# A new table of order, engines and buffers for a two-layer attention kernel

## The chip, the cores and the metric

The kernel runs on one core of one Trainium2 chip. The metric is the device time of one execution in microseconds (us), as the median of several runs. Engines are named as in the profile: PE (matrix multiplication; PEld is its weight load), ACT (activations), DVE (vector), POOL (GpSimd) and SP (which here only issues DMAs).

## The reference, cut to what matters

Four residual layers in a row work on one sequence x of 2048 tokens by 512 features in bf16, with 32 heads of 16 features. Layers 1 and 3 are "A", layers 2 and 4 are "B", with the same weights each time.

```python
x = x + A(layernorm(x)); x = x + B(layernorm(x)); x = x + A(layernorm(x)); x = x + B(layernorm(x))

def A(x, wq, wk, wv, wo, beta):          # four segments of 512 tokens
    for s in range(4):
        p = softmax(qs @ ks.T / 4 + causal mask)          # inside the segment
        a_mem = (phi(qs) @ M) / (phi(qs) @ z + 1e-6)      # memory of the segments before
        o = sigmoid(beta) * a_mem + (1 - sigmoid(beta)) * (p @ vs)
        M = M + phi(ks).T @ vs;  z = z + sum(phi(ks))     # phi(t) = t+1 if t>0 else exp(t)
    return concat(o) @ wo

def B(x, wqkv, w_phi, wo):
    q, k, v = split(x @ wqkv)
    f = lambda t: concat(softmax(t @ w_phi), softmax(-(t @ w_phi)))
    kv = f(k).T @ v;  z = sum(f(k))                       # over all 2048 tokens
    return (f(q) @ kv) / (f(q) @ z + 1e-6) @ wo
```

## The kernel before, in words

The Python code records about 2900 operations in a graph: loads, layer norms, projections, scores, exponentials, evacuations, transposes. Each operation knows what it reads and writes, which engines could run it, and which buffers of which pool it opens. An operation on PE is a group of matmuls (4 to 32 of them), on the other engines one instruction as a rule.

Work is tiled by 128 tokens (a tile) and by 512 tokens (a segment of A, a chunk of B). In A, `a_proj` makes keys, queries and values of a segment: `pair` at L341 splits a projection into two groups of 8 matmuls with 512 columns each (weights `WA_q`, `WA_k`, `WA_v`; on the way out `WA_o`; in B `WB_q`, `WB_k`, `WB_v`, `WB_o`). These are the wide matmuls of the text. `a_att` makes the scores (`D<-pK,pQ`, the diagonal ones with a mask from `tri,rep`), the exponentials on ACT at L351 (`p<-D`, `pP<-D`), and the product with the values (`D<-pW,p` and `D<-pW,pP`, at most 50 columns). All of these and the small products of B (`D<-Rz`, `D<-Rkv`, `D<-MSb`) go through `mm` at L326. The small products are the narrow matmuls of the text. `D` is PSUM: four buffers of 128x1024 f32 that everything PE writes has to share.

B has a barrier of data: `b_query` needs the sums over the keys of all four chunks, which `kv_add` collects. So each B layer has a stretch of wide projections, then `Rz` and `Rkv` products, exponentials and divisions. The next A layer starts on the first tiles that come out.

Transposes are of two kinds. Most are DMAs that SP issues at L364 (`pX<-p` for a normalised input, `p<-p` for an attention output). Those in `PE_T` are done by PE at L380 and evacuated by ACT (L359) or DVE (L360).

Before the first data arrive, PE runs 100 matmuls on a constant (L701, `warm`, `D<-onesb`). Their results are used by nothing.

What sets the order is a table, `ORDER`: a packed list that gives, for all operations, one global order; for each operation its engine; for each buffer its number in its pool. `Graph.place` unpacks it, and `Graph.emit` writes each engine's stream in that order with the semaphore waits that the dependencies and the buffers' reuse need. Nothing reorders at run time: an engine that waits holds up all that stands behind it, and SP's DMAs are issued in the written order too.

```python
raw = zlib.decompress(base64.b85decode("".join(table.split())))
order = [self.ops[i] for i in np.frombuffer(raw, "<u2", n)]
slots = dict(zip(tiles, raw[3 * n:]))
for k, o in enumerate(order):
    o.seq, o.eng = k, ENGS[raw[2 * n + o.id]]
```

Of the kernel before, what the change touches and what calls it, by code (L numbers as in the profile page):

```python
# [16 lines left out]
D = 512  # L17
H = 32
# [42 lines left out]
class Tile:  # L61
# [236 lines left out]
class Kernel:  # L298
# [908 lines left out]
c-q~01C%YvvUWtIvs$OSk8RtwZQHhO+qP}nwr$&fRlCpJnYnk?y!+O_-oMs;xqDYuRz^lfeDOu>tkrRVL1IV_0QI0g5Hx^>&<LVIV`u_Rp&2xXWDp(VLOiGjnV~wAhxkweBxHk<Py<Rq  # L1207
R%ih&p%o~o3AvyGRD^<12y#MeXal987PN&jPzl;W3@8f;pfD7H_Rs-pLs38|1~H*Bl!M~X5n@3d=mec1AtZwAkOQhfUFZ!dAr)BY0=Xdxe1{+K6RN^%2!uD_Krr-yx6l_1e1z067}CHX
0PG3_;3**Xhj-8qy1@__3Q6G^aOe&LAvfm1_wWfm!xtC@d9erdgo%(3d%-l!iNhcl22lp^1H$z%12@2Q3`c`dz)YMA&*23O#t9GvmOemn%m}&IJa`GOU?Y^kuP_|Oz$WO2{V|wAXex|`
qF4+^!Z%m~4n=}3Fb#&_e8|E!!*&<}L(z}6LP?wsJ760`qX9SvRzWHBCx**lCuD)yFbQYEK->iyRs+XbFc||eEzE!^7=%k9I*o<Xum;NGR1|1&5|qUPxEzXLK`e|FFdXK`wJ;3JVLm8>  # L1210
XQ4E%gF?6hD&k5Qj`MH?#-K_V4#vTJ91j675+}oc9EDThFzkl|cmy1bKnLI;B*f7eKt~}MBhnr?2{CCe&cWTV4`*Q_j75>i4`<^7*b9j<KkS1EI0iGpSk$O+F)YO;I2RjW6I_gouo^bR
g_sVSVpLd()$u$mz{6-TB}OKRXJ8fXqKP;T7r}Tez?R{1Jc3nlH>JWxSQ%?z3P_Dru`$NRwOA9Qz(qJf>o5vkfJ+buS5bXT$7*41tcwew9yZ5=6c^LOYKo76R0mt&IoOOXu^G0)E!Y}Q
;wjvSo6sMUV0es&$MFQV!M1n^{4oTh(sc->qZoh@@CNLm^SA@EvIH0rFW@oUircXr?xo|f4WnZkTtk=P3be<A7!5-)Hm#-b)B$(nYCMN~Fa{ojLwFX~;Ck$cJ@5>6!VTD(R$wGNjXg0L
uArTmo@HQdXcxxBmb8*mP-pCd4e26Y!pIm4yJCGxj@>XNMa5Rsi1twpN<}HK0bRzV7>D*#FYJwduqL&o+EkZnQ9FuDQLqjbWc6qX#iQJ;J6?q=cnvyJV!A;$X(@G~tGJ0aQv$k%*YPek
rzX^xhEgXQM$M=%wx=6-6K`P%+<|-8fjUwP8crjqDRrf5^cd4(H@c74X(Yv`6EKRN-~-HxPcb9Dz=!w@vtcGIK$-C+X2;&thk8;kDoCeb5GAB#G=Y{=dc2K~Fas8%@$?+W&^Q`MqbVJB
r~cHJ22ej*M`I}om7pWEo`%q1I!YVp4i=`8l!x7djg*Z|q)C*Wm7-&GoDNYA)`Jey7D`H~X&X(Zt@Ie4KoR<ciRc}D#*8d4drx0*I~8Kz@fGI4T=W+2P(GHM^3V@FOH=48zM<E+gU--h
+DRv<Fnde)=p@~z+famEp=30bp3!M4%F@s&x=P>h9G$02G>x9qbh=Ep=n%`qa<bc$kKW@0I?O&%F?vK<@Dlq>KauDuy}`@uF{Put^om~72TV^#*hf6d($YivK}G2+eW3jGg)&eFmYIE|
($tY9r@`zA{iGpmAmfyuU1NjT3lcPsGSWM|&fM}vFX;xGPYdWKW7L&(W8dfkNy-b~Nzp~hN(WeR%0$4BX<A6xs4O#dkPT%g*f3U(on&RHCmYE|u@P(r^<v#wZ$@l58^g-89;_l8&B{|5
%1*b~ZN}IDR)J2jiqwboW96tX%L6&75@n%dtUo)=j<cCGi)Pb4wx1PaIcO}q!ZK5FHjZ6ol6PWfSP7>1ImX#Nc8AR&!S1tCtTL5klD%R6>>+!=?y^Pnmd$04*hMyvy<&4IfZc>D^q9S7
# [80 lines left out]
```

## Time and profile before

| what | value |
|---|---|
| runs | 456.90, 456.93 and 458.73 us, median 456.93 us |
| span of the profiled execution | 454.8 us |
| PE, PEld, DVE, ACT, POOL busy | 427.2, 289.5, 403.1, 420.9, 58.4 us |
| PE's granted clock | 1.000 over the span |
| instructions | 26184, of them 12085 matmuls and 12085 weight loads |

The profile tells the profiled execution's time as its span, from the first to the last instruction of the program. The median run is 2.1 us longer than this span; that is taken as what lies around the span.

A row of the waits reads: engine, tile and line that waited, what released it, microseconds in total, how often, the longest. A row of the timeline reads: start, length, engine, line, operation, tiles and shape, how many were merged, and in brackets the idle time just before with its releaser. "issue" as releaser means that the engine waited for nothing that the profile shows. A row of the windows reads: the stretch, its length, then for each engine the busy time and in brackets the number of its instructions that lie in it, the clock, the share of DMA and its rate.

### The profile page before, as it was taken

To read this page: it belongs to the slowest core of one execution; us is meant where nothing else is said; L and a number is where in the kernel's file an instruction comes from. 1 tells how busy PE (TensorE), PEld (TensorE's weight loads), DVE (VectorE), ACT (ScalarE), POOL (GpSimd) and SP (SyncE) were. 2 spreads that over 40 slices of the span, in tenths; PEclk is the share of its full clock that TensorE was granted. 3 is DMA by queue.
4 is the path that set the end of the run, shared out by engine and by line. 5 is a ranking of instruction groups with operands and counts; after the bars stand their busy time and mean duration, and the time that the engine had idled before them with its cause. 6 is when DMAs were issued, how large, how long until landed. Compare 5 with 4: busy or idle time off the path is not lost.

```text
span 454.8 us, 26184 instructions
## 1 busy us (share of the span) xinstructions
PE 427.2 (94%) x12085; PEld 289.5 (64%) x12085; DVE 403.1 (89%) x766; ACT 420.9 (93%) x584; POOL 58.4 (13%) x146
## 2 busy tenths in 40 slices
PE   8999999999999989989999998999999988999787
PEld 4756667767766666655556666677677666765444
DVE  7999999998798978869999997999898896788897
ACT  5999999999999997899999999999899999699992
POOL 3411014010101101100330112020020020110000
PEclk9999999999999999999999999999999999999999
DMA  8976655564247212101255668436232414300355
GB/s 251 217 165 100 99 93 109 107 87 80 45 76 111 38 40 50 13 3 27 62 111 86 85 97 103 71 87 81 57 50 49 109 19 63 46 17 4 49 91 180
DMA packets 105167, 36.71 MB, mean 81 GB/s; under 512 B 91730, under 2 KB 105058, under 8 KB 105058
## 3 DMA queue, kind: packets, MB, share of 16 engines
q1 hardware_dynamic: 104226, 34.50, 42.9%
q8 instruction: 95, 1.56, 1.4%
q10 hardware_dynamic: 800, 0.52, 0.4%
q14 instruction: 14, 0.11, 0.1%
q0 software_dynamic: 32, 0.02, 0.0%
HBM read 10.76 MB, written 6.55 MB: 38 GB/s over the span
## 4 chain that ended last, share of the span: by engine, by line
PE 61%; ACT 20%; DVE 12%; issue 3%; DMA 3%; POOL 1%; DVEq 0%
PE D L341 38%; PE D L326 22%; ACT p L351 11%; ACT pP L351 7%; DVE X L961 2%; DVE pQ L686 1%; DVE p L1117 1%; DVE stats L599 1%; DMA pX<-p 1%; DMA p<-p 1%; ACT pS L351 1%; DVE p L620 1%; DMA X<-in_A_x_dram 1%; DVE pK L360 1%; DVE p L906 1%
## 5 line engine op out<-in xcount | busy, mean ns | idle before, releaser
L351 ACT ACTIVATE p<-D 128x1024 bf16<-128x1024 f32 (+1 forms) x256 | 225.6, 934 | 10.8 <-PE D L341 4.9
L351 ACT ACTIVATE pP<-D 128x640 bf16<-128x640 f32 (+2 forms) x192 | 149.5, 828 | 7.2 <-PE D L326 5.9
L326 PE MATMUL D<-pK,pQ 64*128 64x128 bf16 (+6 forms) x1792 | 112.0, 227 | 4.2 <-ACT p L351 1.0
L326 PEld LDWEIGHTS D<-pK,pQ 64*128 64x128 bf16 x1792 | 67.0, 93 | 40.2 <-ACT pP L351 8.5
L326 PE MATMUL D<-pW,pP 64*128 64x50 bf16 (+1 forms) x3072 | 84.0, 181 | 3.4 <-issue 2.7
L326 PEld LDWEIGHTS D<-pW,pP 64*128 64x128 bf16 x3072 | 68.6, 93 | 9.2 <-issue 3.8
L607 POOL TENSOR_SCALAR rstd<-mv 128x1 f32<-128x1 f32 x60 | 17.0, 288 | 340.8 <-DVE mv L600 340.4
L326 PE MATMUL D<-pW,p 64*128 64x50 bf16 (+1 forms) x2048 | 50.4, 181 | 0.4 <-DVE pQ L686 0.2
L326 PEld LDWEIGHTS D<-pW,p 64*128 64x128 bf16 x2048 | 44.3, 93 | 3.9 <-issue 1.1
L599 DVE BATCH_NORM_STATS2 stats<-X 128x6 f32<-128x512 bf16 x63 | 42.3, 679 | 1.9 <-DMA X<-in_A_x_dram 1.6
L961 DVE TENSOR_TENSOR X<-X,D 128x1024 bf16<-128x1024 bf16 (+1 forms) x36 | 39.2, 1096 | 5.1 <-PE D L341 4.6
L326 PE MATMUL D<-tri,rep 64*128 64x64 bf16 (+1 forms) x384 | 40.1, 197 | 0.0
L341 PE MATMUL D<-pX,WA_k 64*128 64x512 bf16 (+1 forms) x288 | 37.4, 353 | 1.0 <-issue 0.5
L341 PE MATMUL D<-pX,WA_q 64*128 64x512 bf16 (+1 forms) x288 | 37.7, 353 | 0.6 <-issue 0.6
L609 POOL TENSOR_TENSOR rstd<-rstd,mhalf 128x1 f32<-128x1 f32 x60 | 35.9, 604 | 3.4
L341 PE MATMUL D<-WB_k,pX 64*128 64x512 bf16 (+1 forms) x288 | 33.8, 352 | 1.1 <-DMA pX<-p 0.4
L341 PE MATMUL D<-WA_o,p 64*128 64x512 bf16 (+1 forms) x288 | 33.2, 352 | 1.6 <-issue 0.8
L1015 DVE TENSOR_REDUCE pS<-p 128x64 f32<-128x1024 bf16 x28 | 33.4, 1211 | 0.9 <-ACT p L351 0.9
L341 PE MATMUL D<-WB_v,pX 64*128 64x512 bf16 (+1 forms) x288 | 33.3, 352 | 0.0
L341 PE MATMUL D<-WA_v,pX 64*128 64x512 bf16 x256 | 33.2, 377 | 0.0
L341 PE MATMUL D<-WB_o,p 64*128 64x512 bf16 (+1 forms) x288 | 32.5, 353 | 0.4 <-ACT p L351 0.3
L341 PE MATMUL D<-pX,WB_q 64*128 64x512 bf16 x256 | 32.5, 376 | 0.3 <-ACT p L351 0.3
(123 smaller groups left out, 665.5 us busy)
## 6 DMA issues: line engine op xcount, KB each, us to landing
v_rows<-pV SPq DMA_DIRECT2D x16, 272.0 KB, 3.6
pW<-v_rows SPq DMA_DIRECT2D x64, 68.0 KB, 2.7
out_dram<-X SPq DMA_DIRECT2D x7, 256.0 KB, 2.6
X<-in_A_x_dram SPq DMA_DIRECT2D x3, 512.0 KB, 7.7
pX<-in_B_wqkv_dram SPq DMA_DIRECT2D x3, 512.0 KB, 4.5
p<-p SPq DMA_TRANSPOSE x73, 3.2
pX<-p SPq DMA_TRANSPOSE x54, 3.6
WA_k<-in_A_wk_dram SPq DMA_DIRECT2D x2, 256.0 KB, 7.2
```

What stands on the lines that cost most here:

```text
L326: ins = e.matmul(out_ap, lhsT, rhs, start=st, stop=sp, tile_position=(basep(lhsT), basep(out_ap)))
L341: ins = e.matmul(out_ap, lhsT[64 * hf:64 * hf + 64], rhs[64 * hf:64 * hf + 64], start=k == 0 and i == 0, stop=k == 1 and i == len(lists[hf ...
L351: return self.g.op({"act": (dur, lambda e: e.activation(out_ap(), in_ap(), func, scale=scale))}, reads, writes, opens, label=label)
L360: "dve": ((340 if fast else n / 0.96 + 65), lambda e: e.tensor_copy(out_ap(), in_ap()))}
L599: v(lambda e: e.bn_stats(self.stats[:, t, :], self.X[:, t, :]), 602, [R("X", t)], [R("st", t)], label="bn")
L607: v(lambda e: e.tensor_scalar(rs, self.mv[:, t, 1:2], LN_EPS, None, op0=ALU.add), 170, [R("mv", t)], [R("rstd", t)], eng="pool", label="rstd")
L609: v(lambda e: e.tensor_tensor(rs, rs, self.mhalf[:], ALU.pow), 540, [R("rstd", t), R("mhalf")], [R("rstd", t)], eng="pool", label="rstd")
L620: v(lambda e: e.tensor_scalar(xn.t[:], self.X[:, t, :], self.mv[:, t, 0:1], self.rstd[:, t:t + 1], op0=ALU.subtract, op1=ALU.mult), 300, [ ...
L686: ch = {"dve": (129 + n / 3.84, lambda e, sl=sl, out=out: e.tensor_scalar(out(), src(), self.m4[:, sl:sl + 1], None, op0=ALU.mult))}
L906: v(lambda e, pvv=pvv, rden=rden, part=part: e.tensor_tensor(part(o).rearrange("p (a h d) -> p a h d", a=2, h=16), pvv()[:, :, :, 0:16], r ...
L961: self.v(lambda e: e.tensor_tensor(X(), X(), src(), ALU.add), 65 + 512 * n / 0.96, pr + xr, xr, label="res")
L1015: v(lambda e, E=E, k=k, Z=Z: e.tensor_reduce(Z.t[:, 64 * k:64 * k + 64], E.t[:].rearrange("p (a f h) -> p a h f", a=16, h=4), AX.X, ALU.ad ...
```

## The change

Only the table `ORDER` is replaced. The code around it and the operations are the same.

```diff
 ORDER = """
-c-q~01C%YvvUWtIvs$OSk8RtwZQHhO+qP}nwr$&fRlCpJnYnk?y!+O_-oMs;xqDYuRz^lfeDOu>tkrRVL1IV_0QI0g5Hx^>&<LVIV`u_Rp&2xXWDp(VLOiGjnV~wAhxkweBxHk<Py<Rq
...
+c-q}q1DGvIvd)M|SG)V#wr$(CZQHhO+qP}nw(VEvoI5i+v-4(mpT2Kjoi1c$X5f!MqB1)+OT?10WGoI#z_PGtEGi?$SZ0=xNtTU8XGvIMmXpP0@mPG8hh=5CSUHxRWn#ryc~*iUE5Hh}s;nBT&PuWx
...
 """
```

On the large scale the order stays: the same layers, segments and chunks follow each other in the same way, and groups move by a few places. Twenty operations change their engine. From ACT to DVE go three evacuations of transposed inputs, one evacuation of a value projection of B, two of transposed outputs and two maskings of keys; from DVE to ACT go four evacuations (one of keys, one of queries, one of values, one of a transposed output) and one masking. Seven memsets and fills move between POOL and DVE, all in the first 25 us.

At the start of PE's stream, the warm-ups (`onesb`) before the change are spread between the four transposes of normalised inputs (`ident,p`) and the first projections:

```order
L701 MATMUL D<-onesb 128x256 x8
L380 MATMUL D<-ident,p 128x64 x8
L701 MATMUL D<-onesb 128x512 x4
L380 MATMUL D<-ident,p 128x64 x8
L701 MATMUL D<-onesb 128x512 x2
L380 MATMUL D<-ident,p 128x64 x8
L701 MATMUL D<-onesb 128x512 x4
L380 MATMUL D<-ident,p 128x64 x8
L341 MATMUL D<-pX,WA_k 128x256
```

After it, at the same place:

```order
L701 MATMUL D<-onesb 128x256 x8
L701 MATMUL D<-onesb 128x512 x18
L380 MATMUL D<-ident,p 128x64 x8
L701 MATMUL D<-onesb 128x512 x2
L380 MATMUL D<-ident,p 128x64 x8
L701 MATMUL D<-onesb 128x512 x4
L326 MATMUL D<-beta_sb,onesb 128x32
L380 MATMUL D<-ident,p 128x64 x16
L341 MATMUL D<-pX,WA_k 128x256
```

Nine groups of warm-ups now stand ahead of the first transpose, and none is left between the first projections, where eight matmuls of them stood.

The second place is PE's stream in the third segment of the second A layer, around 321 us of the profile. Before, 52 narrow matmuls in one piece, two diagonal scores, 12 more narrow ones, and then the projection of queries:

```order
L326 MATMUL D<-pW,pP 128x50 x52
L326 MATMUL D<-pK,pQ 128x192 x2
L326 MATMUL D<-pK,pQ 128x64 x2
L326 MATMUL D<-pK,pQ 128x128 x2
L326 MATMUL D<-tri,rep 128x2x32 x2
L326 MATMUL D<-pK,pQ 128x224 x2
L326 MATMUL D<-pK,pQ 128x96 x2
L326 MATMUL D<-pK,pQ 128x128 x2
L326 MATMUL D<-tri,rep 128x2x32 x2
L326 MATMUL D<-pW,pP 128x50 x12
L341 MATMUL D<-pX,WA_q 128x512 x8
L326 MATMUL D<-pK,pQ 128x256 x4
```

After, in PE's stream at the same place:

```order
L326 MATMUL D<-pW,pP 128x50 x64
L341 MATMUL D<-pX,WA_q 128x512 x8
L326 MATMUL D<-pK,pQ 128x224 x2
L326 MATMUL D<-pK,pQ 128x96 x2
L326 MATMUL D<-pK,pQ 128x128 x2
L326 MATMUL D<-tri,rep 128x2x32 x2
L326 MATMUL D<-pW,pP 128x50 x20
L326 MATMUL D<-pK,pQ 128x256 x4
L341 MATMUL D<-pX,WA_q 128x512 x8
```

The first half of the projection (eight wide matmuls) has moved up, so that 16 wide matmuls instead of 8 stand within the same count of matmuls.

The third place is SP's queue where it issues the transposes of the first chunk's input of B (`pX1`) between 63 and 82 us. Before:

```order
L364 DMA_TRANSPOSE pX1<-p14 128x4x128
L364 DMA_TRANSPOSE pX1<-p16 128x4x128
L462 DMA pX2<-in_B_wqkv_dram 128x4x512
L364 DMA_TRANSPOSE pX0<-pX2 128x4x128
L368 DMA pW1<-v_rows 32x8x136 x2
```

After:

```order
L364 DMA_TRANSPOSE pX1<-p10 128x4x128
L462 DMA WB_o<-in_B_wo_dram 64x1x512
L364 DMA_TRANSPOSE pX1<-p12 128x4x128
L368 DMA pW1<-v_rows 32x8x136 x2
L364 DMA_TRANSPOSE p11<-p25 128x4x128
L462 DMA WB_o<-in_B_wo_dram 64x1x512
```

A load of a weight piece now stands between the first two of the four transposes.

More of the change, by code (lines that the diff above doesn't have):

```diff
@@ L1211 @@
[L1211 to L1218, printed above, removed]
@@ L1259 @@
[L1259 to L1261 removed]
+c-q}q1DGvIvd)M|SG)V#wr$(CZQHhO+qP}nw(VEvoI5i+v-4(mpT2Kjoi1c$X5f!MqB1)+OT?10WGoI#z_PGtEGi?$SZ0=xNtTU8XGvIMmXpP0@mPG8hh=5CSUHxRWn#ryc~*iUE5Hh}s;nBT&PuWx
@@ new lines @@
+tQ4!s3bDehG^@ZWvRbSNQw&&LR*%(Z4Om0gh&5(SSX0)FHD@hYOV*0DW^Gto){eDj9au-!iFIaOSXb7Km0{gkQPzX?WGPr#mXcLsm04|8hgl|=VVngphZSSJSZ~&c#bBD{U{zQu_KkgKAJ|70ll@=}
+2C_kHFzd^PFo1rnKO4Yau_x>``@}x8H|#AN$uh9?>?wQ4azIWf0_)g%RusmwTrd@K!!$q$WD!^p3t{is2KJ2QXV2MaHi5lh8`&H-8K%QrHU(zDJT{6=VPDvAHjyo6shPzfe95A)uWTyI19_nYY-7cs
+Burx?STN3JW7tv_6_>E$&=<C|i9pZ~CczH2k}YF7X*uJth^=BPn1JMLFa*L7*vz)DO>8UM$<DG+wwvu@d)Qv)&(5%5HkQp~7J^_L8^(sRU~q6Xi-rTC5R`&4P#T6p0muhsAwQIZNvt50hr%$K4T8Ba
+4A!vzFb@Vm1*iyX*+>`;huC4ZkL_o(m;*=Hd^UqkXCq(~%!UN80usU;2!WO02M1VY%0-DlLVhw(fKD+5;ZZ{<oMzE62FAp+l!YSTJ{SWNU<vGpnJ^2+!Xh{Xdtfn)gT^o#4nq^z3n`!~%!m3=4I02s
@@ new lines @@
+91ja&0fb;EW@LW2fGve(P#Jb%N@xhxp$asD8W0OoK}5_=kuWReW&7~}HiMP83Y$Y378%pBFw8>*sSstO+-xE9$Jh`D(ouTKKx?2b)P@$&6k5V2SPQM79@K)GPzQEnYiI-cSUPrr#e<{lBHIjmFfN3H
+OKby#hhuP=9b^$85*%ZZAppZ58pMaZ6afAZktK$6tP-4O$-$3B!6eWYVqsE94dE~lmqRkx2*=?BY=L!f63)X}*bZA^HLi!<a1M6C5jX?e-~g<_qi_(SLOZy|uCw;g0an2&I1S5jHLSoExD$3jOKgR$
+F*<aF3vdy-Ll5W#Q6M?i!}{0&Q{Y}~i2JZQc7~qN1$seB><Yah23&%)kPf;*IMxT!LmG$)v9Si$#5Pz9>tI`qgS9atEXFJBDqDglSzU~aiSROX!uHq<ui_QBhRty!UWHBA5j$f$ypBz=F*d<QI1D@B
+Be;P>a5xUd$B+Rs!W~G6Cs-HkikaXp6s8`S1+qdmxCYPR3G~GLI0AcN0elKCU?ld&dvG5T-~-4`*P$SG!y9lDvO{9bNVgz0_Q$a}9+%=M?1!Uq9QMHhxE2TEGAxdLaUCAUF*q0p;SpSqC2#^x#7P*L
@@ new lines @@
+-Dct0LpX_>@exack6Ao?3CCG{d<GlvC~m`&7{(&8+t3{gVPTw%$M7I-!PmGQKf)(Cgl{kveui)G1-?U0%!NBJ4d%wTcpBf~DZGux@eF>%yLbmb;XT}nC-5>}!72C@pW#$|13v)qEWUzsm<Oj}UVIH-
+VJ>C{hWU{2JkG=UxBwsFO?;0J@jJeQ4|oeN;tza+kMR<|#P^UEU*SRe0EZ|YUZhKu9>3sye2$;-0lvV)#PJ9XqQR5}1$LpYc%8oC4eCloC<hhAWSA67VJ0eu7w{&_N15?00G7rgC{f{6(zu_l(E(bB
+jDV)2!Ayvh6|-R(8bIx-2bHCP)RQ_;IXX_mXao(X{xpO}Qa?ID-DoJ4#|n6oy3;8dMZKsu9i=`rn)=dB%7_&x16IT_G?r%IOq_+s=oS^Fy(IZQQoI-yr`cEu%is-G4$I;q%#K7ka1P#Lm+1lBr*m|d
+t`Mht)RAt}9ePQxNKh$~RFYoPLpnnjXbwH5v-F1MQe`|(^Qa0gpwl#;6jen{{!|T1ljb#PAsNp3BYHxDPoRlZi=NUm3ZN-8mC92n849EzvQ(Qo(Nda3%V{!oreF%Ah!l<@(JY!x57;!CPRq#h#Wa&<
@@ L1262 @@
+!(|XEm+zsj8gHdQ3URY300KQWl4ocrC+&_1Ca)-R*%<0V;$es<6<rO=pS+L0I_ZKzzMZw#1W)FLdad&<Vm*GjCCj>$)h?!fKX>0QLkzmff!=ID9_Sb1#xvMMO<z)IcV;LH@MM6;6W2GF7_Rh?K<>ig
+#xoGT+R006S8I^<8bCgyQMj3G!d#t}0z7rb11hl)*D;RDTLauvt6&UuD}@BFPLE{)ZiM~3g~R)bT*qaor^*EhuRd?O8jC#GgIADiBRGoOY81#J#3<KPZz%i%JTqM>VdR<TMpc63TDWFom>XC($lO&8
+j<FH~6$Wc2J?IHeDg?RlWQk>NF>@f;o0A^?y1C=h{XYOp&F7Z
 """
```

82 lines of the change are left out of this document (36 added, 46 removed).

## The prediction

> **What bounds the kernel now.** I read the page first: busy shares, the chain that ended last, the DMA queues.
>
> ```profile
> span 454.8 us, 26184 instructions
> PE 427.2 (94%) x12085; PEld 289.5 (64%) x12085; DVE 403.1 (89%) x766; ACT 420.9 (93%) x584; POOL 58.4 (13%) x146
> q8 instruction: 95, 1.56, 1.4%
> PE 61%; ACT 20%; DVE 12%; issue 3%; DMA 3%; POOL 1%; DVEq 0%
> ```
>
> PE and ACT are both about full, and the chain changes between them: 61% of it is PE, 20% ACT. All operations stay, so only waits can go. The third row is the one to remember: a queue of the kind "instruction" moved 95 packets. PE's stream is 12085 weight loads, 12085 matmuls and some 140 waits, and 95 times 256 is 24320. So one packet carries about 256 instructions of PE, or 128 matmuls with their loads. I call that a block.
>
> Second, the waits of PE's two rows of work.
>
> ```profile
> PEld D L326 <- ACT pP L351: 10.4, 34, 1.1
> PEld D L326 <- ACT p L351: 9.7, 29, 0.8
> PEld D L326 <- issue: 8.8, 17, 1.7
> PEld D L341 <- issue: 8.8, 23, 1.0
> PE D L326 <- issue: 4.9, 7, 1.6
> PE D L341 <- issue: 2.5, 5, 0.8
> ```
>
> Weight loads stand still for 20.1 us because an exponential is late, and for 17.6 us, 40 times, on "issue": nothing that the profile shows holds them. Queued matmuls cover most of that; 12 such stalls reach the matmuls and make 7.4 us of idle PE. Third, the timeline of PE shows where these stand.
>
> ```profile
> 162.52 0.61 PE L341 MATMUL D<-pT,p 64*128 64x68 bf16 x28 [0.33 <-issue]
> 203.57 0.21 PE L326 MATMUL D<-Rz,p 64*128 64x32 bf16 x4 [0.46 <-issue]
> 260.24 0.80 PE L341 MATMUL D<-pX,WA_k 64*128 64x512 bf16 x5 [0.52 <-issue]
> 281.12 0.27 PE L326 MATMUL D<-pW,pP 64*128 64x50 bf16 x8 [0.78 <-issue]
> 323.54 0.37 PE L341 MATMUL D<-pX,WA_q 64*128 64x512 bf16 x1 [0.62 <-issue]
> 386.03 1.34 PE L341 MATMUL D<-WA_o,p 64*128 64x512 bf16 x8 [0.84 <-issue]
> 424.77 0.24 PE L326 MATMUL D<-Rz,p 64*128 64x48 bf16 x7 [1.55 <-issue]
> ```
>
> They fall inside a group of equal matmuls, between two that wait for the same things: the queries' projection is cut after seven of eight at 323.54. Fourth, the windows that end at a stall, with one that has none.
>
> ```profile
> 162.51:166.52 4.01, 3.09 (x128) 2.43 (x128) 2.98 (x3) 3.56 (x6) 0.00 (x0) 1.00 0.20 40
> 200.58:203.56 2.98, 2.06 (x140) 1.84 (x132) 1.86 (x5) 2.81 (x5) 0.00 (x0) 1.00 0.02 5
> 256.24:260.23 3.99, 3.48 (x129) 2.75 (x128) 3.96 (x8) 3.89 (x6) 0.00 (x0) 1.00 0.65 85
> 276.98:281.11 4.13, 3.05 (x134) 2.21 (x129) 3.45 (x10) 3.91 (x5) 1.12 (x3) 1.00 0.87 126
> 319.80:323.53 3.73, 3.12 (x129) 2.39 (x128) 3.59 (x7) 3.33 (x5) 0.79 (x2) 1.00 0.46 90
> 396.00:418.00 22.00, 22.00 (x374) 14.21 (x371) 19.29 (x35) 20.27 (x32) 1.57 (x4) 1.00 0.12 15
> ```
>
> The first window runs from one stall to the next and holds 128 matmuls and 128 loads, one block. The next four were laid over one block each, counted in PE's order; each ends in a stall after 3.0 to 4.1 us. So the next block is not there sooner than that, and PE stands when its work for 128 matmuls is shorter. Such a block is one with few wide matmuls. This bounds PE from outside, and moving matmuls between blocks changes it. The last window, without stalls, is a B layer's projections: PE is never idle there, ACT is.
>
> [...]
>
> **The change, part by part.** First, the start.
>
> ```profile
> 1.11 5.58 PE L701 MATMUL D<-onesb 64*128 64x512 bf16 x76 [1.11 <-DVE onesb L531]
> 7.39 0.29 PE L380 MATMUL D<-ident,p 64*128 64x64 bf16 x8 [0.69 <-DVE p L620]
> 9.24 0.27 PE L341 MATMUL D<-pX,WA_k 64*128 64x256 bf16 x1
> ...
> 13.42 0.38 PE L701 MATMUL D<-onesb 64*128 64x512 bf16 x2
> ...
> 214.04 1.03 PE L341 MATMUL D<-WB_o,p 64*128 64x512 bf16 x8
> 214.91 0.63 PE L326 MATMUL D<-Rkv,p 64*128 64x64 bf16 x32
> ...
> 4.43 0.69 DVE L599 BATCH_NORM_STATS2 stats<-X 128x6 f32<-128x512 bf16 x1 [1.57 <-DMA X<-in_A_x_dram]
> ...
> 12.41 1.33 ACT L688 ACTIVATE pQ<-p,m 128x512 bf16<-128x512 bf16 x2
> 14.30 2.23 ACT L351 ACTIVATE pP<-D 128x768 bf16<-128x768 f32 x3
> ```
>
> A matmul of 512 columns takes 0.109 us (eight of them from 214.04 to 214.91). The 76 warm-ups end at 6.69 by their row; 18 more take 2.0 us behind them, less the last one's modelled tail of some 0.2. So the first transpose starts at about 8.4, not 7.39. Behind it six warm-ups stand instead of ten, and two of the evacuations go to DVE beside ACT, so I put the first projection at about 9.5 instead of 9.24. From there the 64 projection matmuls ran 4.18 us, to 13.42, with six of the eight warm-ups between (0.65; the last two are the row at 13.42); without them they end at about 13.0: 0.4 us sooner. ACT masks one key block there instead of two (1.33 us for both, so 0.62 us less ahead of its evacuation). The first exponential moves from 14.30 to about 13.6. **Start: -0.7 us**, between 0 (the loads then set the pace) and -1.2. The memsets that change engine lie ahead of DVE's first input at 4.43, where it waits 1.57 us for data; that hides them. Without that cover the gain of the start would be lost to them: the end 0.
>
> Second, the blocks. The price of a narrow matmul from spacing in the timeline:
>
> ```profile
> 281.45 0.26 PE L326 MATMUL D<-pW,p 64*128 64x50 bf16 x8
> 281.55 0.23 PE L326 MATMUL D<-pW,pP 64*128 64x50 bf16 x6
> ```
>
> Eight wide ones take 0.87 us, eight narrow ones 0.10 (281.45 to 281.55): eight wide ones in place of eight narrow ones make a block 0.77 us longer. In the new order the block that ended in the stall at 203.57 has 8 wide ones for none, that at 260.24 has 19 for 12, that at 281.12 has 8 for none, that at 323.54 has 16 for 8. Each gains about what its stall was, so I take these four as gone: 0.46 + 0.52 + 0.78 + 0.62 = 2.4 us. At 386.03 four value products and a score now stand ahead of the `WA_o` group, which also waited for its data: 0.4 of the 0.84 us. The blocks at 162.5, 166.5 and 424.8 are as short as before (none, 8 and none wide): their stalls stay. In the count of all 94 whole blocks, 17 instead of 18 have under ten wide ones and 6 instead of 9 have under four. Four others get longer and four get shorter by a group; the worst new one stands before 218 us (8 for 16) and could stall for some 0.6 us, the mean of the twelve. I set these against each other. PE then loses 2.8 us less.
>
> Does PE's time reach the end? In the four windows ACT was busy 2.81 of 2.98, 3.89 of 3.99, 3.91 of 4.13 and 3.33 of 3.73 us: it has only 0.9 us of room there. What PE gains beyond that waits for ACT next, unless it is used in stretches like 396 to 418, where PE alone sets the pace and ACT had 1.7 us to spare. Ends: -0.9 (ACT's room alone), and -4.3 (the 17.6 us of load stalls shrink by a quarter, as the time by which blocks fall short of 3.6 us does, from 21 to 17 us by these prices). **Blocks: -2.4 us**, nearer to the four rows than to the estimate over all.
>
> Third, the engines. Behind the start, four evacuations leave ACT and four come.
>
> ```profile
> L359 ACT ACTIVATE pX<-D 128x512 bf16<-128x512 bf16 x10 | 5.7, 596 | 1.3 <-PE D L380 1.3
> ...
> L359 ACT ACTIVATE pV<-D 128x1024 bf16<-128x1024 f32 x3 | 3.2, 1064 | 0.0
> ```
>
> Two of those that come have 1024 columns (1.06 us each), one of those that leave; the other five have 512 and are near 0.6. ACT's work changes by about +0.5 us and DVE's by as little, and I set **0**, ends -0.5 and +0.5. At the end of the kernel PE's groups are the same: 0.
>
> Sum: -0.7 - 2.4 + 0 = -3.1 us against the span of 454.8, so 451.7. The runs' median lies 2.1 us above the span, so 456.93 - 3.1 = **453.8 us**.
>
> **The rivals.**
>
> More: all load stalls shrink, -0.7 - 4.3 - 0.5 = -5.5, 451.4 us. For it speaks that the relieved blocks lie in both A layers; against it that most load stalls are covered. ACT takes over: PE waits as long for `p` and `pP` as it waited for instructions. Then only ACT's room counts: -0.9 and half the start, 455.7 us. For it: the 20.1 us. Against it: 61% of the chain is PE. [...]
>
> Slower: a transpose comes late in SP's queue.
>
> ```profile
> 66.28 4.52 DMA pX<-p
> 70.89 1.04 PE L341 MATMUL D<-WB_k,pX 64*128 64x512 bf16 x8 [0.41 <-DMA pX<-p]
> 21.20 0.67 SPq L462 DMA_DIRECT2D WB_o<-in_B_wo_dram  x1
> 82.95 1.19 SPq L364 DMA_TRANSPOSE p<-p  x1
> ```
>
> SP issues in the written order, a transpose takes it 1.2 us, and the key projection at 70.89 already waited for one. In the new order a load of 0.67 us stands between the two transposes that this group needs, so it would start at about 71.6. Elsewhere, a needed transpose behind one more transpose comes 1.2 us later. Three of these uncovered eat the gain of 3.1; from five on the kernel is over 0.5% slower: -3.1 + 5 x 1.2 = +2.9, 459.8 us. For it: many transposes stand in another order. Against it: of all PE rows shown, this is the only one told to have waited for a DMA, and it waited 0.41 us, so elsewhere there is cover.
>
> **How the numbers follow.** Forecast 0.43, more 0.13, ACT 0.22, the page's rule 0.07, slower 0.15. What a measurement of this kernel can tell from no change is about 0.5%, 2.3 us: under 454.6 is faster, over 459.2 slower. Forecast and more are faster (0.56), ACT and the rule the same (0.29), slower 0.15. The range reaches from a little under the case "more", 450.3, to the case "slower" without its last places, 458.6; it leaves out the tails of these two. The forecast's own range is 452.5 to 455.3 (blocks from -0.9 to -3.7).
>
> **What would show each step.** Right: fewer than 12 stalls of PE's matmuls on "issue", about 5 us together, none in the groups named, those at about 162, 166 and 424 still there; the first `pP` exponential at about 13.6. Wrong: "issue" falls while the waits for `p` and `pP` grow by as much (ACT); a new stall just before 218; PE's waits for `pX<-p` or `p<-p` over 3 us (slower). The prediction is wrong as a whole if PE's stalls move to other blocks instead of going.

## The result and the profile after

| | time | runs |
|---|---|---|
| before | 457.31 us median (456.90 to 458.73) | 4 |
| after | 472.79 us median (472.58 to 477.32) | 4 |
| forecast | 453.8 us, range 450.3 to 458.6 | |

The change makes the kernel slower: ratio 1.0362, 95% interval 1.0307 to 1.0417, about 16 us. The span of the profiled execution grew from 454.8 to 471.0 us. The page after, the rows that answer to those of before:

```profile
span 471.0 us, 26155 instructions
PE 437.7 (93%) x12085; PEld 283.3 (60%) x12085; DVE 404.1 (86%) x774; ACT 421.3 (89%) x581; POOL 54.2 (12%) x141
q8 instruction: 95, 1.56, 1.4%
PE 65%; ACT 13%; DVE 12%; DMA 4%; SPq 3%; issue 3%; DVEq 0%
```

The work of ACT and DVE is nearly what it was; both have more idle time. PE is busy 10.5 us longer with the same 12085 matmuls. The chain has 4 points more of PE, 7 less of ACT, and SP's queue is in it now. The waits of PE, after:

```profile
PEld D L341 <- PE D L341: 27.1, 66, 0.6
...
PEld D L326 <- ACT p L351: 9.5, 25, 1.3
PEld D L326 <- ACT pP L351: 8.9, 31, 0.7
PEld D L341 <- issue: 8.9, 23, 1.5
...
PEld D L341 <- DMA pX<-p: 5.4, 4, 3.7
PEld D L326 <- DMA pW<-v_rows: 3.6, 3, 1.8
PEld D L326 <- issue: 3.5, 12, 0.5
...
PE D L341 <- issue: 1.8, 3, 0.8
...
PE D L326 <- issue: 0.6, 2, 0.4
```

and two rows of the same view before, which the prediction had not shown:

```profile
PEld D L341 <- PE D L341: 2.2, 5, 0.6
...
PEld D L341 <- DMA pX<-p: 0.6, 2, 0.3
```

The forecast gain is there: idle time of PE's matmuls on "issue" fell from 7.4 us in 12 stalls to 2.4 us in 5. It is even larger than these rows tell, because "issue" also stands where the view names no releaser. Counted through PE's stream (weight loads, matmuls and the waits that are instructions of their own), 11 of the 12 stalls before stand 189 to 192 instructions behind a multiple of 256: these are stalls at block borders, 7.1 us in sum. After, only three stand there, 0.8 us. The other two are at groups that wait for a transpose: 0.77 us at 75.52, where it landed at 75.43, and 0.79 us at 79.43, where it landed at 79.34.

But the first row is new. PE's weight loads wait 66 times for PE's own matmuls, where they waited 5 times before. In `pair`, the second half of a projection adds to the same part of `D` as the first half, from the other 64 rows of the array, so `hard=o1` makes it wait until the first half has ended. No run here leaves the wait out of this form, so the traces show its price, not what it is needed for. Before, another group stood between the halves 153 times in 158, and hid the wait; after, 66 second halves stand directly behind their first. The timeline shows what that costs:

```profile
95.76 1.04 PE L341 MATMUL D<-WA_o,p 64*128 64x512 bf16 x8
96.86 1.04 PE L341 MATMUL D<-WA_o,p 64*128 64x512 bf16 x8
```

The second half starts 1.10 us after the first; eight wide matmuls took 0.87 (the prediction's rows at 214.04 and 214.91). So a direct pair (a second half right behind its first) costs 0.23 us, and 61 more of them some 14 us.

Where the time was lost shows in the first and last start of the same groups, before and then after (minimum, median and maximum duration in ns, first and last start in us):

```profile
L341 PE MATMUL D<-WA_o,p x288: 266/376/387, 54.7 to 399.4; 64*128 64x512 bf16 x112, 64*128 64x256 bf16 x32
L341 PE MATMUL D<-pX,WB_q x256: 372/376/387, 177.1 to 430.7; 64*128 64x512 bf16 x128
```
```profile
L341 PE MATMUL D<-WA_o,p x288: 267/376/387, 60.3 to 413.7; 64*128 64x512 bf16 x112, 64*128 64x256 bf16 x32
L341 PE MATMUL D<-pX,WB_q x256: 372/376/387, 185.0 to 447.0; 64*128 64x512 bf16 x128
```

The new kernel is 5.6 us late at 55 us, 7.9 at 177, 14.3 at 399 and 16.3 at 431: a loss at the start, and then one spread over the whole kernel. The matmuls themselves did not become slower (376 ns in both).

**The start.** Windows before and after, first of the kernel before and then of the new one (the count in brackets after PE's busy time is that of its matmuls):

```profile
2.00:4.00 2.00, 2.00 (x12) 0.68 (x10) 0.86 (x1) 1.13 (x1) 1.81 (x8) 1.00 0.94 292
4.00:6.00 2.00, 2.00 (x50) 1.09 (x48) 1.54 (x5) 1.51 (x4) 0.00 (x0) 1.00 0.85 239
```
```profile
2.00:4.00 2.00, 2.00 (x12) 0.74 (x10) 1.94 (x7) 1.13 (x1) 1.54 (x5) 1.00 0.94 289
4.00:6.00 2.00, 2.00 (x12) 0.77 (x10) 1.97 (x9) 1.74 (x5) 0.00 (x0) 1.00 1.02 290
```

Until 4 us both run the wide warm-ups at one in some 0.2 us, half the later speed, though the granted clock is told as 1.00. Before, this ended at 4.0 us; in this execution of the new kernel it went on to 6.2. Then the rows of PE, ACT and SP, after, and SP before:

```profile
1.15 8.58 PE L701 MATMUL D<-onesb 64*128 64x512 bf16 x94 [1.15 <-DVE onesb L531]
9.56 0.28 PE L380 MATMUL D<-ident,p 64*128 64x64 bf16 x8
...
28.57 1.04 PE L341 MATMUL D<-pX,WA_k 64*128 64x512 bf16 x8 [3.48 <-ACT p L351]
...
15.54 1.72 ACT L351 ACTIVATE pP<-D 128x896 bf16<-128x896 f32 x2
...
13.72 1.28 SPq L364 DMA_TRANSPOSE pX<-p  x1
...
19.36 1.23 SPq L364 DMA_TRANSPOSE pX<-p  x1
...
21.27 1.34 SPq L364 DMA_TRANSPOSE pX<-p  x1
...
23.63 1.27 SPq L364 DMA_TRANSPOSE pX<-p  x1
```
```profile
12.38 1.29 SPq L364 DMA_TRANSPOSE pX<-p  x1
...
14.89 3.58 SPq L364 DMA_TRANSPOSE pX<-p  x2
...
19.25 1.91 SPq L364 DMA_TRANSPOSE pX<-p  x1
```

The first transpose of PE starts at 9.56 instead of 7.39. DVE's two evacuations wait for it, the next segment's layer norm stands behind them, and its four transposes are issued up to 23.63 instead of 19.25. PE's `WA_k` group at 28.57 then stood 3.48 us. The row names ACT's `p`, but the exponential that the group waits for had ended at 24.8; the group's other waits are for the four transposes, the last of which landed at 28.4.

**A balance of PE's time.** Over all 1165 groups I took the spacing from each group's start to the next, less the lower quartile for its kind (398.4 us in sum). The rest I put down to what the next group waited for, or to the inside of the group. In us, for runs told of below as well:

| kernel | own first half | inside a group | waits with a DMA among them | ACT | DVE | other |
|---|---|---|---|---|---|---|
| before | 1.1 | 19.1 | 8.5 | 13.3 | 9.4 | -0.1 |
| after | 15.2 | 8.1 | 17.0 | 17.6 | 7.1 | 2.9 |
| a_sep | 0.7 | 14.9 | 17.6 | 23.2 | 14.3 | 2.6 |
| a_pe | 7.6 | 10.4 | 13.5 | 21.4 | 9.1 | 1.7 |
| a_three | 6.0 | 13.4 | 14.0 | 19.9 | 9.2 | 1.2 |
| b_shift | 1.2 | 34.5 | 8.6 | 14.5 | 10.1 | 3.5 |

After against before: +14.1 for the halves, -11.0 inside groups (the block stalls, and load stalls that reach matmuls), +8.5 at waits that have a DMA among them, +4.3 ACT, -2.3 DVE, +3.0 other: +16.6 us. The balance is accounting, not a cause; the runs below test the causes.

### The profile page after: what moved, and what is told of

Read it like the earlier page. It is cut to its first block, busy times and chain, and to the rows that moved or that the text cites. A ratio compares the mean times of both kernels' runs of the same rounds, so it can differ in the third digit from the quotient of the medians.

```text
span 471.0 us, 26155 instructions
## 1 busy us (share of the span) xinstructions
PE 437.7 (93%) x12085; PEld 283.3 (60%) x12085; DVE 404.1 (86%) x774; ACT 421.3 (89%) x581; POOL 54.2 (12%) x141
## 4 chain that ended last, share of the span: by engine, by line
PE 65%; ACT 13%; DVE 12%; DMA 4%; SPq 3%; issue 3%; DVEq 0%
PE D L341 41%; PE D L326 21%; ACT p L351 8%; ACT pP L351 4%; SPq L364 3%; DMA pX<-p 3%; PE D L701 2%; DVE p L835 1%; DVE X L961 1%; ACT pS L351 1%; DMA p<-p 1%; DVE p L1117 1%; DVE pT L360 1%; DVE p L906 1%; DVE pQ L686 1%
## 5 line engine op out<-in xcount | busy, mean ns | idle before, releaser
L351 ACT ACTIVATE pP<-D 128x768 bf16<-128x768 f32 (+2 forms) x192 | 148.9, 818 | 11.4 <-PE D L326 9.8
L326 PE MATMUL D<-pK,pQ 64*128 64x128 bf16 (+6 forms) x1792 | 109.3, 227 | 3.3 <-ACT pP L351 1.9
L326 PE MATMUL D<-pW,pP 64*128 64x50 bf16 (+1 forms) x3072 | 85.0, 181 | 3.6 <-DMA pW<-v_rows 2.8
L326 PEld LDWEIGHTS D<-pK,pQ 64*128 64x128 bf16 x1792 | 64.4, 93 | 34.5 <-ACT pP L351 6.1
L607 POOL TENSOR_SCALAR rstd<-mv 128x1 f32<-128x1 f32 x60 | 14.7, 249 | 354.7 <-DVE mv L600 354.6
L326 PE MATMUL D<-pW,p 64*128 64x50 bf16 (+1 forms) x2048 | 49.0, 181 | 0.9 <-ACT pP L351 0.4
L326 PEld LDWEIGHTS D<-pW,p 64*128 64x128 bf16 x2048 | 43.3, 93 | 3.5 <-issue 1.1
L609 POOL TENSOR_TENSOR rstd<-rstd,mhalf 128x1 f32<-128x1 f32 x60 | 34.7, 585 | 3.5
```

Of the source, the lines that this page charges most:

```text
L326: ins = e.matmul(out_ap, lhsT, rhs, start=st, stop=sp, tile_position=(basep(lhsT), basep(out_ap)))
L351: return self.g.op({"act": (dur, lambda e: e.activation(out_ap(), in_ap(), func, scale=scale))}, reads, writes, opens, label=label)
L607: v(lambda e: e.tensor_scalar(rs, self.mv[:, t, 1:2], LN_EPS, None, op0=ALU.add), 170, [R("mv", t)], [R("rstd", t)], eng="pool", label="rstd")
L609: v(lambda e: e.tensor_tensor(rs, rs, self.mhalf[:], ALU.pow), 540, [R("rstd", t), R("mhalf")], [R("rstd", t)], eng="pool", label="rstd")
```

## The experiments

The kernels below ran in five sessions, two to four of them at a time, each session on one chip with the kernel before beside them. The median of before was 457.8 to 459.6 us in these sessions, so I compare ratios to it: the change has 1.0362, and 0.01 of ratio is 4.6 us. The theories in the expectations: A, PE's waits for its own first halves; B, late transposes alone; C, the start and late steps of SP's queue; D, something else in the table holds the time.

### Halves moved apart and together

a_sep, a row that stands for the 52 moves (order of PE, after against a_sep):

```diff
+L341 MATMUL D<-WA_v,pX 128x512 x8
 L326 MATMUL D<-pK,pQ 128x224 x2
 L326 MATMUL D<-pK,pQ 128x96 x2
 L326 MATMUL D<-pK,pQ 128x128 x2
 L326 MATMUL D<-tri,rep 128x2x32 x2
-L341 MATMUL D<-WA_v,pX 128x512 x16
+L341 MATMUL D<-WA_v,pX 128x512 x8
```

> The changed kernel, with 63 of the 66 second halves of a projection that stand directly behind their first half moved apart by one or two groups of PE (52 swaps of neighbours in PE's order; the order of every other engine, the engines and the buffers stay as in the changed kernel). Theory A (the wait of a second half for its own first half costs PE 0.23 us each time): 63 x 0.23 = 14.5 us less than the changed kernel's 472.8, so about 458, with 3 waits of the kind PEld D L341 <- PE D L341 left. Rival B (the loss is late transposes and loads, the self-waits are covered by queued matmuls): 470 to 473, waits for DMAs as long as before.

Measured: ratio 1.0423 (1.0386 to 1.0461). Not one microsecond came back, against theory A. The balance shows what became of the 14.5 us: ACT +5.6, DVE +7.2, inside groups +6.8. By the two orders, 15 groups that are no halves went behind a half, nine of them scores that an exponential waits for; behind eight wide matmuls that is 0.87 us later. And at one place a transpose that had been just in time was late:

```profile
343.08 1.04 PE L341 MATMUL D<-WA_o,p 64*128 64x512 bf16 x8 [2.00 <-DMA p<-p]
```

PE's clock has a part in it too. The trace of a_sep shows a granted clock of 0.50 for 3.4 us from 30.0, from 344.1 and from 446.5 us, each behind a stall of PE (2.64, 2.00 and 1.18 us). The eight wide matmuls that start at 30.81 there took 1.68 us until the next group, not 0.87. By an estimate from these numbers (three times 3.4 us at half the clock) the three can cost PE 5 us; the trace of the changed kernel has no record of 0.50 ahead of 470.4 us, at its end. So this run took the waits away and put others in; it does not decide.

b_adj, the same the other way round:

```diff
-L341 MATMUL D<-WA_v,pX 128x512 x8
-L326 MATMUL D<-pK,pQ 128x256 x4
-L341 MATMUL D<-WA_v,pX 128x512 x8
-L326 MATMUL D<-pK,pQ 128x256 x4
+L341 MATMUL D<-WA_v,pX 128x512 x16
+L326 MATMUL D<-pK,pQ 128x256 x8
```

> The kernel before, with 54 more second halves put directly behind their first halves (59 instead of 5), the group that stood between moved behind or ahead; nothing else moved. Theory A: 54 x 0.23 = 12.4 us more than 456.9, so about 469, up to 475 because 39 of the moved groups are scores that now come 0.87 us later. Rival B: under 460.

Measured: ratio 1.0455 (1.041 to 1.05), 21 us, above the range of A. It agrees with A, but here too scores came late, so the price of the wait alone is not shown.

a_full and b_full take the wait away with another form of the projection: a half now uses all 128 rows of the array for its own part of `D`, each matmul cut into two of half the columns (the main lines):

```diff
+        full = label not in ("KV", "M")
...
+                if full:
+                    for i, (out_ap, lhsT, rhs) in enumerate(ab[k]):
+                        for c in range(2):
...
+                    return ins
...
         o1 = self.g.op({"pe": (dur, half(0))}, reads, writes, opens, label=label, rows=64)
-        return self.g.op({"pe": (dur, half(1))}, reads, writes, label=label + "2", rows=64, hard=o1)
+        return self.g.op({"pe": (dur, half(1))}, reads, writes, label=label + "2", rows=64, hard=None if full else o1)
```

> The changed kernel's table, but projections use all 128 rows of the array (each matmul cut into two of half the columns, so that the number of instructions stays), so a second half writes another half of D than the first and needs no wait for it; the small products KV and M keep the two-row-group form and their waits (17 of the 66). Theory A: 49 x 0.23 = 11.3 us less, so about 461.5, if the full-row form itself costs nothing; the same form on the table before says what it costs. Rival B: 472 to 473.

> The kernel before with the same full-row projections: control for the form. Theory A: only the 5 self-waits go (3 of them are projections), under 1 us, so 456 to 457 plus what the form costs. Rival B: the same. If it is slower by some us, the form costs that, and is to be subtracted from the run with the changed table.

Measured: a_full 1.0569 (1.0528 to 1.061), b_full 1.0545 (1.0504 to 1.0586). The form costs 25 us, for which none of the theories had a figure. Its waits in b_full:

```profile
PEld D L326 <- issue: 31.6, 127, 1.7
PEld D L341 <- issue: 14.9, 64, 0.7
```

191 load stalls on "issue" instead of 40, 46.5 us instead of 17.6. In this form PE goes back and forth between 64-row and 128-row groups; no run here changes that alone, so its share of the 25 us is not shown. With 46 fewer additional self-waits the two tables are 0.2% apart instead of 3.6. That speaks for A, but PE is the bound of everything in this form (busy for 95% of the span in a_full, 96% in b_full), so it is weak evidence.

### One suspect at a time

b_wait keeps every order of before and adds the waits (`DRAIN` lists the 61 first halves):

```diff
-            deps = dict.fromkeys(sorted(o.deps, key=lambda d: d.id))
+            deps = dict.fromkeys(sorted(o.deps, key=lambda d: d.id)); drain = prog[e][-2] if e == 'pe' and len(prog[e]) > 1 and prog[e][-2].id in DRAIN else None; deps.update({drain: None} if drain else {})
...
-            cand = [d for d in deps if (d is o.hard or not (d.kind == "c" and d.eng == "pe" and e == "pe")) and not covers(kn, d)]
+            cand = [d for d in deps if (d is o.hard or d is drain or not (d.kind == "c" and d.eng == "pe" and e == "pe")) and not covers(kn, d)]
```

> The kernel before with its table as it is; in addition the group that follows the first half of a projection waits for that half's end, for the 61 pairs whose halves stand directly behind each other in the changed kernel only (the second half's own wait then finds it done). No order changes. Theory A (waits of PE for its own matmuls made the change slower, 0.23 us each): 61 x 0.23 = 14 us more, 469 to 472. Theory C (SP's queue and the start made it slower; the self-waits fall into time in which PE would have waited for ACT or for instructions): under 462.

Measured: ratio 1.032 (1.0276 to 1.0364), 14.6 us for 61 waits, 0.24 us each. This is what A said, and no operation moved. Its rows:

```profile
PEld D L341 <- PE D L341: 12.1, 34, 0.6
PEld D L326 <- PE D L341: 11.5, 24, 0.6
...
PE D L326 <- issue: 9.4, 13, 1.6
...
PE D L341 <- issue: 2.3, 4, 1.0
```

The loads wait 58 times, 23.6 us in sum, instead of 5 times and 2.2 us. But the waits were not all that was added. PE's stream has 178 waits that are instructions of their own instead of 141 (145 in the changed kernel), so the block borders lie up to 37 instructions earlier in its work. The last two rows show stalls on "issue" of 11.7 us in 17 instead of 7.4 in 12. So up to 4.3 of the 14.6 us can be these, and the 61 waits are worth 10.3 to 14.6 us, 0.17 to 0.24 each. That such waits make up most of what the change costs is shown on the order of before. That they fell into waiting time in the changed table is not excluded by this run.

a_sp moves DMA steps in SP's queue:

```diff
+L364 DMA_TRANSPOSE pX1<-p16 128x4x128
 L462 DMA X<-in_A_x_dram 128x4x512
-L364 DMA_TRANSPOSE pX1<-p16 128x4x128
-L368 DMA v_rows<-pV1 128x2x544
 L364 DMA_TRANSPOSE pX1<-p17 128x4x128
-L462 DMA WB_o<-in_B_wo_dram 64x1x512
 L364 DMA_TRANSPOSE pX1<-p18 128x4x128
+L368 DMA v_rows<-pV1 128x2x544
+L462 DMA WB_o<-in_B_wo_dram 64x1x512
```

> The changed kernel with 16 DMA steps moved forward in SP's queue, to where their source was ready in the changed kernel's trace (transposes and gathers behind which PE waited at 28.6, 75.5, 79.4, 112.1, 287.4, 333.1 and 406.9 us); all other engines, engines of operations and buffers stay. Theory C: of the 11.0 us that PE waited at these seven places, those of the start stay in part (its sources are late), the others go: 6 to 9 us less than 472.8, so about 465. Theory A: the late DMAs lie beside the self-waits and nothing is won, 471 to 473.

Measured: ratio 1.0463 (1.04 to 1.0525), a miss. The waits at 75.5, 79.4 and 112.1 went, but another step had become late:

```profile
100.39 1.04 PE L341 MATMUL D<-WA_o,p 64*128 64x512 bf16 x8 [3.37 <-DMA p<-p]
```

SP issues in the written order, so every step moved forward moves others back, by 1.2 us a transpose (in the changed kernel 1.19 at least, median 1.27). The queue of the changed kernel shows how tight it is, near 330 us:

```profile
328.81 1.80 SPq L368 DMA_DIRECT2D v_rows<-pV  x1
330.65 2.60 SPq L368 DMA_DIRECT2D pW<-v_rows  x3
333.30 1.20 SPq L364 DMA_TRANSPOSE p<-p  x1
...
335.15 1.87 SPq L364 DMA_TRANSPOSE p<-p  x1
```

The sources of the two transposes were ready at 325.1 and 331.3; they were issued at 333.30 and 335.15, behind gathers that wait for the store at 328.81 to land. The later one landed 0.5 us before PE started the group that needs them (338.36 and 338.87); in a_sep the two came 2.00 us too late for this group, and in a_sp 2.15.

b_start and a_start exchange the first 16 us:

```diff
-L380 MATMUL D<-ident,p 128x64 x8
-L701 MATMUL D<-onesb 128x512 x4
+L701 MATMUL D<-onesb 128x512 x18
 L380 MATMUL D<-ident,p 128x64 x8
```

> The kernel before, with the changed kernel's order and engines for what starts in its first 16 us (132 operations), its own for the rest. Theory C: PE stood 3.65 us at 28.6 us in the changed kernel, since the second segment's normalised tiles came 2.6 us later; the whole kernel then is 3 to 5 us longer, 460 to 462. Theory A: the start has one pair of self-waits, 457 to 458.

Measured: 1.014 (1.0095 to 1.0186), 6.4 us. More than the 3 to 5 of theory C. The seam between the two orders may add some of its own (8 direct halves instead of 5 are 0.7 us); how much is not shown.

> The changed kernel with the order and engines of before for what starts in the first 16 us, its own for the rest, SP's queue behind that unchanged. Theory C (the start costs 3 to 4 us): 468.5 to 470. Theory A: 472 to 473.

Measured: 1.025 (1.0194 to 1.0306), 5.1 us less than the change. Both say the start costs 5 to 6 us.

> The changed kernel with the order and engines of before for the first 16 us, and 13 of the DMA steps moved forward as in a_sp. Theory C: the start (4) and SP's queue (6 to 8) come back, 460 to 463. Theory A: 468 to 473, since the 66 self-waits stay.

Measured: 1.0409 (1.0332 to 1.0485). A miss: the start won was lost again, in part to the same displaced steps as in a_sp (the `WA_o` groups there waited 2.79 and 1.71 us in this run).

### Fewer direct halves, without new late work

a_pe, a_search and b_search move groups by a few places, each move kept only where by the measured durations nothing else came late. For instance in a_pe:

```diff
-L326 MATMUL D<-pW,pP 128x50 x40
+L326 MATMUL D<-pW,pP 128x50 x60
 L380 MATMUL D<-ident,p 128x64 x8
-L326 MATMUL D<-pW,pP 128x50 x28
+L326 MATMUL D<-pW,pP 128x50 x8
```

> The changed kernel with 62 of PE's 1165 groups moved by one to five places, so that 33 instead of 66 second halves stand directly behind their first half; the moves were kept only where, by the durations measured in the traces so far, no exponential or evacuation becomes late. All other engines' orders stay. Theory A (self-waits, 0.23 us each): 33 x 0.23 = 7.6 us less than 472.8 at best, 3 to 7 after what the moves cost: 466 to 470. Theory D (in the changed table the self-waits only fill time in which PE would wait for something else): 472 or more, as with the 63 pairs moved apart before.

Measured: 1.0245 (1.0202 to 1.0287), 5.3 us less than the change, for 33 direct halves less. Theory A said 3 to 7, D none. This speaks for A in the changed table too, and against D. It is no proof: the 62 moves changed other waits as well (in the balance the halves fell by 7.6 us, waits with a DMA by 3.5, while ACT rose by 3.8).

> The changed kernel after the same kind of local moves on all queues: 50 groups of PE, 6 instructions of ACT, 34 of DVE and 23 DMA steps of SP moved by a few places; 27 second halves stand directly behind their first half. Theories A and C together: 39 x 0.23 = 9 us, and up to 5 of the time that PE waits for late transposes: 458 to 465. Theory D: 470 or more.

Measured: 1.0184 (1.0109 to 1.0259), 8 us less, at the upper end of what A and C said (465 by its ratio); the interval is 7 us wide.

> The kernel before after the same kind of local moves: 28 groups of PE, 7 instructions of ACT, 22 of DVE and 11 DMA steps moved; still 5 direct second halves. All theories: the price of a move is read from the same durations, so if waits for late data and for own matmuls are what counts, 2 to 6 us less than before, 451 to 455; if instruction blocks or something not in those durations decide, 456 to 460.

Measured: 0.9951 (0.9919 to 0.9982), about 2 us less than before. With b_two it is the fastest kernel of the study, but the difference is at the bound of what a measurement can tell.

### Together, and the borders

> The changed kernel with all three suspects reduced at once: before's order and engines for the first 16 us, 72 groups of PE and 30 DMA steps of SP moved by a few places (26 instead of 66 direct second halves); ACT's and DVE's orders behind 16 us stay as in the changed kernel. Theories A and C together, added up: 40 x 0.23 = 9 us, the start 4 to 5, and 1 to 3 of the late DMAs: a ratio to before of 1.000 to 1.012, 457 to 462. Theory D (something else in the changed table holds it at 470, and each cure only uncovers it): over 1.018, 465 or more.

Measured: 1.0193 (1.0134 to 1.0252). 8 us came back, 11 to 16 were expected. The ratio lies just over the 1.018 that was named for D, and its interval reaches to both sides. In the balance the halves cost 9.2 us less and DMA waits 3.0, while the insides of groups cost 5.3 more, ACT 2.3 and DVE 2.1: the cures uncover other waits, as D had it. Block stalls are only a part of that. At the borders they rose from 0.8 to 2.9 us; another 5.1 us that the view puts down to "issue" stand at groups that wait for a DMA.

> As the run above, and also 10 instructions of ACT and 44 of DVE moved by a few places (26 direct second halves). Theories A and C: a little faster than the run above, a ratio of 0.997 to 1.010, 455 to 461. Theory D: 465 or more.

Measured: 1.0189 (1.0136 to 1.0241), the same, and again just over D's 1.018: the moves of ACT and DVE won nothing more.

> The kernel before with 48 groups of PE, 9 instructions of ACT, 33 of DVE and 16 DMA steps moved by a few places, kept where they shorten the waits by the measured durations even if every DMA lands 0.6 or 1.2 us later; 4 direct second halves. Theories A and C (own waits and late data set the time): at least as fast as the first such kernel (ratio 0.995), 0.988 to 0.995, 451.5 to 454.5. If instruction blocks or chance decide: 0.995 to 1.003.

Measured: 0.9957 (0.9922 to 0.9992), as b_search.

b_shift and a_shift change one number in `warm`:

```diff
-                for rows, n, m in ((64, 51, 12), (64, 64, 8), (64, 256, 4)):
+                for rows, n, m in ((64, 51, 44), (64, 64, 8), (64, 256, 4)):
```

> The kernel before with 64 more matmuls of 51 columns among its first warm-ups, so that all borders of PE's instruction blocks lie 64 matmuls, half a block, earlier in its work; nothing else changes. Block theory: the stalls of matmuls on issue at about 162, 166, 204, 260, 281, 323, 386 and 425 us go or move to other groups, and the time changes by some us either way (451 to 463). Rival (the stalls belong to those groups, whatever the count of instructions): the same eight stalls, and 456 to 458.

Measured: 1.0401 (1.0356 to 1.0446), 18 us slower by 64 narrow matmuls. The waits:

```profile
PE D L326 <- issue: 20.0, 25, 2.2
...
PE D L341 <- issue: 2.8, 2, 2.0
```

22.8 us in 27 stalls instead of 7.4 in 12, and in other groups: those in the groups at 162.5, 166.5 and 203.6 are gone, new ones of 1.0 to 1.5 us stand at 128.9, 137.5 and 152.0. Of the 27, 26 stand 191 or 192 instructions behind a multiple of 256, as before, though the work there is another. So the stalls belong to the count of instructions, not to the groups, and the order of before suits its borders. The 64 matmuls themselves are not the cause: the first transpose came 0.3 us later (7.69 instead of 7.39). But three of the long stalls in this run (2.01, 2.16 and 1.77 us) have a stretch of 3.4 us at clock 0.50 beside them, as in a_sep, so a part of the 18 us is PE's clock.

> The changed kernel with 64 more matmuls of 51 columns among its first warm-ups: all block borders half a block earlier, as done with the kernel before. Block theory: the changed table has few stalls on issue (2.4 us of PE's matmuls) because its order suits the borders; with borders elsewhere they rise to over 12 us and the time by 8 to 18, 481 to 491. Rival (its few stalls come from its 66 self-waits, which make every block longer, wherever the borders lie): under 6 us of stalls, 472 to 477.

Measured: 1.0571 (1.0514 to 1.0628), 9.6 us slower than the change. PE's stalls:

```profile
PE D L326 <- issue: 8.1, 11, 1.7
...
PE D L341 <- issue: 2.8, 3, 1.5
```

10.9 us instead of 2.4: a little under the 12 expected, far over the rival's 6. So most of the relief came from the order around the borders. That they stay below b_shift's 22.8 may come from the 66 self-waits, which make blocks longer; a_sep, with 3 self-waits, has 2.8 us of stalls at the borders, against 0.8 in the changed kernel.

> The kernel before with 54 groups of PE, 12 instructions of ACT, 31 of DVE and 11 DMA steps moved by a few places, this time kept only where they help with a block of PE's instructions taking at least 3.9 us, the figure that fits both the kernel before and the one whose borders were moved. Theory (own waits, late data and blocks together set the time): faster than the two searched kernels before it, a ratio of 0.983 to 0.993, 449 to 454. Rival (what is left is not in these durations): 0.994 to 1.000.

Measured: 0.9987 (0.9957 to 1.0017): no difference, as the rival said. Moves that count on 3.9 us for a block won nothing.

## Why the prediction was wrong, point by point

- **The step that failed is "so only waits can go": the sum has no term for PE waiting for PE.** Behind the start it has the blocks and the engines (0), and puts PE's wait for its own first half at nothing, without a reason. The change set 61 more second halves directly behind their first. The row that prices this, 2.2 us in 5, stood in the waits of before, and PE's whole order had the pairs as one row of x16 in place of two of x8. b_wait gives the term: +14.6 us where the sum had none, at least 10.3 of it the waits themselves.
- **Start: -0.7 forecast, +5 to +6 measured** (a_start, b_start). The first transpose was put at 8.4 and came at 9.56; the first exponential at 13.6 and came at 15.54. The price of the 18 warm-ups was right: they took 1.94 us (7.62 to 9.56), 0.108 each. What failed is that the 76 ahead of them would end where they ended before. PE's half speed lasted 2.9 us in the trace of before and 5.1 in this one, so they ended 1.1 us later. That part is chance: a_pe has the same warm-ups, its half speed lasted 3.3 us, and its first transpose came at 8.67, near the forecast. The larger part is not chance: b_start and a_start give 5 to 6 us over several executions. The memsets were the wrong cover to ask for: behind the first transpose stand DVE's evacuations, the layer norm and SP's transposes. The end 0 of the range was no bound.
- **Blocks: -2.4 forecast, -5.0 in matmuls' stalls on "issue" measured, -6.3 at the borders alone.** That the stalls stand at block borders was right, shown by the shifted borders (26 of 27 stalls in b_shift), and the size was too small by half or more. "None in the groups named" held; "about 5 us together" did not, it was 2.4, and of the three that should stay, only the one at 162.5 is left, with 0.22 us. But "PE stands when its work for 128 matmuls is shorter" than 3.0 to 4.1 us is no clean rule: before, blocks of 2.8 and 2.9 us (to 49.7 and to 105.0) passed without a stall of the matmuls.
- **Does PE's time reach the end?** In the main it did. b_wait put some 14 us of waits and 4.3 us of stalls on PE and lost 14.6; b_shift put on 15.4 us of stalls and lost 18. "ACT takes over" would have covered a larger part.
- **The rival "slower"** had its chance of 0.15 on late transposes. They came, also at the place that it named: the second transpose for `WB_k` was issued at 71.76, behind the load, and the group stood 0.77 us for it, about the 0.67 us of the load. Waits with a DMA among them took 8.5 us more in the balance, so its price, three to five of 1.2 us, was too low. By the same balance that is less than the 11.0 us that the insides of groups gave back, so alone it would not have made the kernel 16 us slower. What the case given 0.07 rested on is shown by no run here; in b_shift PE's matmuls stood 22.8 us on "issue", nearly all of it at borders.
- **Open:** the runs with all three causes reduced stay 8 to 9 us above before. Their balance puts that on ACT, DMA and the remaining 26 direct halves; no run takes these apart. No run puts back only the buffer numbers, or the eight evacuations that change engine behind the start. No run leaves only the second half's wait out of the changed kernel; there its price rests on a_pe, for 33 of 66.

## What to carry to other kernels

Before costing a new order, list every wait an engine has for itself, and count in the new order how often nothing stands in between: here one such wait was worth 0.17 to 0.24 us, and 61 of them 10.3 us or more (b_wait). A cover has to be priced too; what was hidden before is free only as long as it is hidden, and in a tuned order almost nothing is idle by chance. When PE's stream is near full (94% before) and its matmuls are narrow, treat the count of instructions as part of the schedule: 64 matmuls of 51 columns at the start moved the borders and cost 18 us (b_shift). Added waits can move them too: 37 of those in b_wait are instructions of their own.

## What the runs showed of the hardware

- PE's stalls on "issue" stand at one place in every 256 instructions, whatever the work there (11 of 12 before, 26 of 27 in b_shift); half a block of shift was worth 18 us of 457 (before) and 9.6 of 473 (after). I had expected stalls to be worth single microseconds. No clean threshold is shown: the blocks that ended in a stall lasted 2.9 to 5.3 us before, and some of 2.8 and 2.9 us passed without one.
- PE's first matmuls ran at half speed for 2.9 us before and 5.1 us after, with the granted clock told as 1.00; the traces' record of the clock begins only at 4.0 and 6.2 us. The moment at which the full speed came varied: over the 20 profiled executions of these kernels it was 2.5 to 5.5 us after the first matmul.
- In 14 of the 20 traces the granted clock falls to 0.50 for 3.4 us ahead of the program's end, 25 times in all, each time within 2 us of a stall of PE of 1.0 to 3.9 us. In such a stretch eight wide matmuls took 1.68 us, not 0.87 (a_sep, at 30.81). Not every such stall had one beside it: the stall of 3.48 us at 28.57 in the changed kernel was followed by none.
- Projections over 128 rows among groups over 64 rows cost 25 us, with 191 load stalls instead of 40 and the same number of matmuls (b_full).
